# An mLSTM cell followed by a gated MLP on one core: a reordered head, shorter denominators, and seven products for eight in the last chunk

## The chip, the core and the metric

The kernel runs on one core of one Trainium2 chip. The metric is the device time of one execution in microseconds (us); lower is better. Each time below is one of three runs of the kernel before, or belongs to the one execution that the profiler recorded.

The engines are named as in the profile: PE is TensorE (matrix products; PEld its weight loads), DVE is VectorE, ACT is ScalarE, POOL is GpSimd, SP is SyncE, which here does nothing but issue DMA transfers. "Lnnn" is a line of the kernel before, unless a line of the new kernel is meant, which is then said.

## The reference

```python
# q, k, v, o_gate: (4, 8, 768, 40); i_gate, f_gate: (4, 8, 768)
for t in range(S):
    m_new = np.maximum(f_gate[:, :, t] + m, i_gate[:, :, t])
    f_stab = np.exp(f_gate[:, :, t] + m - m_new)
    i_stab = np.exp(i_gate[:, :, t] - m_new)
    m = m_new
    C = f_stab[..., None, None] * C + i_stab[..., None, None] * np.einsum('bhd,bhe->bhde', vt, kt)
    n = f_stab[..., None] * n + i_stab[..., None] * kt
    h_tilde = np.einsum('bhde,bhe->bhd', C, qt)
    denom = np.maximum(np.abs(np.einsum('bhd,bhd->bh', n, qt)[..., None]), 1.0)
    y[:, :, t] = sigmoid(o_gate[:, :, t]) * h_tilde / denom
x = y.transpose(0, 2, 1, 3).reshape(3072, 320)
h = x @ w_in                 # w_in: (320, 2048)
out = (h * np.cos(h)) @ w_out  # w_out: (2048, 320)
```

The two weight matrices arrive as float64 and are made float32 in the kernel from their bits.

## The kernel before

**Cells and chunks.** The 768 steps are cut into 6 chunks of 128 (`c` = 0 to 5), and a chunk into 4 cells, one for each batch entry `b`; cell `n` is chunk `n // 4`, batch `n % 4`, with its 8 heads. A cell turns the recurrence into matrix work: `scores` (L492, keys times queries), `weigh` (L498, times the decays `E`), `values` (L518 to L527, times the values, plus the state carried over times the scaled queries `qG`), `denominators` and `divide` (the normalisation and the output gate), and `seam` and `state`, which bring the state to the next chunk. The four cells of a chunk give `xT[c]` (320 features in 128 + 128 rows, and the remaining 64 twice in `xL[c]`) for the 512 columns of the chunk.

**The MLP.** `Up(c, f2)` makes 256 of the 2048 hidden features for the 512 columns, in two PSUM banks (`pup`, one for `e` = 0, one for `e` = 1): four products over the two 128-row parts (L667, each two instructions) and two over the last 64 rows (L661). Then ACT makes `near` (L675, to integer), DVE `rest` (L678), ACT the sine (L683), DVE `gate` (L687). The banks come free with the last read of `gate`. `down` (L699, chunk 0) or a scheme of 7 products for 8 (L848, chunks 1 to 5, with sums of halves made by DVE and POOL in `sums`, L736 to L744) multiplies the gates by `w_out`.

**The order of the work** is written out by hand: every engine runs its instructions in the order in which the Python text records them. `first_cells` does cells 0 to 3 while data still arrive; `first_period` does cell 4 beside `Up(0, 0)` and `Up(0, 1)`; then `both_parts(c, b)` does the cell `(c + 1) * 4 + b` beside the two slots `f2 = 2b` and `2b + 1` of chunk `c`. A slot is: `Up`, `near`, `rest`, (half a cell), sine and `gate`, and a run of down products. Chunk 5 has no cell beside it.

**Weights.** `w_in` comes in four blocks of 512 features (two slots each), a block in three pieces: `weights_in(f)` issues 4 + 4 transfers of 128 KB (L141) for two 128-row pieces and 4 of 64 KB (L179) for the last rows. `w_out` comes in eight pieces of 640 KB (L185), one for each slot. A piece is made float32 by ACT (`take_apart`, L153 and L155), DVE (`bound`, L159 and L160; then L166) and POOL (`put_together`, L167). `bound` is a clamp and a pair of shifts, both `tensor_scalar` in place. Pieces wait in three (`w_out`) or four (`w_in`) staging buffers called `bits`; a transfer into a buffer waits until POOL has read the piece before it.

**DMA.** SP issues nearly all transfers, one after the other; an instruction there that waits holds all later transfers. Transfers are counted on eight semaphores in turn, so that a transfer also waits for the one eight before it (some of these belong to `seam_out`'s `xL` transfers, which ACT issues, L626). For a cell SP brings `E` (512 KB, broadcast, L369), and for two cells at once the raw queries and keys (L341), `G` (the decays of the state, L358), and keys and values in rows (L346). `load_o` brings the output gates of a chunk (8 transfers of 80 KB, L311), which `sigmoid` (L320, L322) turns; `low_dimensions` (L455, ACT) moves 8 of 40 dimensions of raw queries and keys before DVE can turn them in blocks (`turn_blocks`, L465).

**Normalisation of a turned cell.** `turn_gate` (L470) turns the output gates on DVE; `denominators` (L541, L542) takes max(|d|, 1) over 128 x 128; `divide` multiplies values by gates (L548), takes 128 x 128 reciprocals (L549), spreads two rows over three tiles by three shuffles (L552) and multiplies (L556).

**The gates' tables.** `gates_turn` turns the gate factors of chunks 1 to 5 on PE (L275) after cell 3's values and adds one product (L276); `gates_keep` copies both to SBUF. `clear_low` (L448) sets two raw tiles to zero by POOL in `first_period`. `warm(k)` runs k products (L920) whose results nobody reads.

Of the kernel before, what the change touches and what calls it, by code (L numbers as in the profile page):

```python
# [29 lines left out]
def kernel(  # L30
# [20 lines left out]
    nc = tc.nc  # L51
# [68 lines left out]


# [35 lines left out]
    def bound(dst):  # L157
        t = dst.bitcast(I32)
        nc.vector.tensor_scalar(out=dst, in0=dst, scalar1=LEAST, scalar2=GREATEST, op0=OP.max, op1=OP.min)  # L159
        nc.vector.tensor_scalar(out=t, in0=t, scalar1=5, scalar2=2, op0=OP.logical_shift_left,  # L160
                                op1=OP.logical_shift_right)
# [96 lines left out]
    def gates_exp():  # L258
        for e in (eG, eW):
            nc.scalar.activation(out=e, in_=e, func=AF.Exp)  # L260
        dst = G_d.rearrange("(c j q) s -> j q c s", c=R, j=2)
        for j in range(2):
            nc.gpsimd.dma_start(out=dst[j], in_=eG[j:BH:2])
# [6 lines left out]
    def gates_turn():  # L270
        pg = ps_o.tile([128, R, 2, BH], FP, name="pg", tag="o")
        pd = ps_o.tile([128, R - 1, BH], FP, name="pd", tag="o")
        for c in range(R):
            for j, src in enumerate((a1, eW)):
                nc.tensor.transpose(pg[:, c, j], src[:, c], ident[0:BH, 0:BH])  # L275
        nc.tensor.matmul(pd.rearrange("p c b -> p (c b)"), one.to_broadcast([BH, 128]), dd.rearrange("r c b -> r (c b)"),  # L276
                         start=True, stop=True)
        return pg, pd

    def gates_keep(pg, pd):  # L280
        nc.scalar.copy(out=tab[:, 1:NC, 0:2], in_=pg)
        nc.scalar.copy(out=tab[:, 1:R, 3], in_=pd)
# [163 lines left out]
    def clear_low():  # L446
        for w in "qk":
            nc.gpsimd.memset(raws[w][1], 0.0)  # L448
# [17 lines left out]

    def turn_gate(n):
        c, b = divmod(n, B)
        oTs[n] = p1.tile([128, 3, C], FP, name="oT", tag="oT")
        nc.vector.transpose(out=oTs[n].rearrange("q g (t k) -> q g k t", t=32), in_=sig[c][:, b].rearrange("q (g k) i -> q g k i", g=3))  # L470
# [67 lines left out]
    def denominators(n):  # L538
        vt = heads_of[n]
        dn = dns[n] = p2.tile([128, C], FP, name="dt", tag="dt")  # L540
        nc.vector.tensor_scalar(out=dn, in0=vt[:, 2], scalar1=-TWO_PI, scalar2=TWO_PI, op0=OP.mult, op1=OP.max)  # L541
        nc.vector.scalar_tensor_tensor(out=dn, in0=vt[:, 2], scalar=TWO_PI, in1=dn, op0=OP.mult, op1=OP.max)  # L542

    def divide(n):
        c, b = divmod(n, B)
        vt, dn = heads_of[n], dns[n]
        yt = vt if n == B else p1.tile([128, 3, C], FP, name="yt", tag="yt")
        nc.vector.tensor_tensor(out=yt, in0=vt, in1=oTs[n], op=OP.mult)  # L548
        nc.vector.reciprocal(out=dn, in_=dn)  # L549
        db = p1.tile([128, 3, C], FP, name="db", tag="db")  # L550
        for i, mask in enumerate(([FROM0] * 32, [FROM1] * 32, [FROM0] * 16 + [FROM1] * 16)):
            nc.vector.stream_shuffle(out=db[:, i], in_=dn, mask=mask)  # L552
        if b == 0:
            new_x(c)

        nc.vector.tensor_tensor(out=xT[c][:, NK * b:NK * b + NK + 1], in0=yt, in1=db, op=OP.mult)  # L556
        ys[n] = xT[c][:, NK * b + NK]
# [91 lines left out]
    class Up:  # L649
# [35 lines left out]
        def gate(self, e):  # L685
            g = gp.tile([128, B * C], FP, name="g", tag="g")
            nc.vector.scalar_tensor_tensor(out=g, in0=self.pu[e], scalar=TWO_PI, in1=self.n[e].bitcast(FP),  # L687
                                           op0=OP.mult, op1=OP.mult)
            gs[self.c, 2 * self.f2 + e] = g
# [155 lines left out]
    def run(made, n):  # L845
        for _ in range(n):
            a, lhs, rhs, start, stop = next(made)
            nc.tensor.matmul(a, lhs, rhs, start=start, stop=stop)  # L848
# [39 lines left out]

    def down_slot(c, f2):

        if c == 0:
            if f2 > 0:
                down(0, f2 - 1)
            return
        if f2 == 0:
            if c == 1:
                down(0, LAST)
            else:
                run(made_of[c - 1], 12)
            return  # L900
        if f2 == 1 and c > 1:
            run(late_products(c - 1), NF)
            combine_late(c - 1)
            return
        if c not in made_of:
            made_of[c] = all_products(c) if c < NC - 1 else last_products()
        each = 14 if c == NC - 1 else 12
        quota = [0] * 8
        for m in range(2, 8):
            quota[m] = each * 7 * (m - 1) // 6 - each * 7 * (m - 2) // 6  # L910
        if c == NC - 1:
            quota = [0, 0, 14, 14, 14, 14, 14, 21]
        run(made_of[c], each if c == 1 else quota[f2])
# [8 lines left out]
    def first_cells():  # L922
        nc.vector.memset(nil, 0.0)
        gates_in()
        nc.scalar.copy(out=ident_b, in_=ident)
        load(0, "qk")
# [27 lines left out]
        pieces.extend(weights_in(0))  # L954
# [16 lines left out]
        values(0)  # L971
        normalize(0)
        scores(1)
        gates_exp()
        turn(2)
        turn_out(2, False)
        warm(2)
        seam(0)
        weigh(1)
        seam_out(0)  # L980
        state(0)
        load_two(B, "qk")
# [5 lines left out]
        load_M(B)  # L988
        outs.append((0, weights_out(0)))
# [24 lines left out]
        pg = gates_turn()  # L1014
        warm(2)
        more = weights_in(1)
        pieces.append(next(more))
        load_G(B)
        load_two(B, "Kv")
# [6 lines left out]
        bound(pieces[0][0])  # L1026
        put_together(*pieces.pop(0))
        gates_keep(*pg)
        pieces.extend(more)
        load_M(B + 1)  # L1030
# [3 lines left out]
        load_E(B + 2)  # L1034
        low_dimensions(B)
# [5 lines left out]
        odd_values(B)  # L1041
# [17 lines left out]
    def first_period():  # L1059
# [16 lines left out]
        for some in pieces:  # L1076
            take_apart(*some)
        out_of_psum(n)
        bound(piece[0])
        put_together(*piece)  # L1080
        load_out(p)
        up = Up(0, 1)
        for dst, bits in pieces:
            bound(dst)
            put_together(dst, bits)
        pieces.clear()
        for e in range(2):
            up.near(e)
# [12 lines left out]
        clear_low()  # L1101
# [3 lines left out]
        load_out(p)  # L1105
# [3 lines left out]
        turn_gate(n)  # L1109
# [3 lines left out]
        pieces.extend(weights_in(2))  # L1113
        load_two(n + 2)
        load_E(n + 3)
# [6 lines left out]
    def both_parts(c, b):  # L1122
# [3 lines left out]
        for i in range(2):  # L1126
            f2 = 2 * b + i
            up = Up(c, f2)
# [9 lines left out]
            if i == 0:  # L1138
# [14 lines left out]
                if c == 0:  # L1153
                    made = [pieces.pop(0) for _ in range(min(1, len(pieces)))]
                    p, piece = outs.pop(0)
                    made.append(piece)
                    for dst, bits in made:
                        take_apart(dst, bits)
                    for dst, bits in made:
                        bound(dst)  # L1160
                    for dst, bits in made:
                        put_together(dst, bits)
                    load_out(p)
# [27 lines left out]
            if cell and i == 0:  # L1191
                turn_gate(n)
                values(n)
                seam(n)
                normalize_turned(n)
                fade(n)
# [14 lines left out]
            if i == 1:  # L1211
# [14 lines left out]
                if (c, f2) == (0, LAST):  # L1226
                    weight_sums(0)

# [39 lines left out]
```

## Time and profile before

| what | value |
|---|---|
| three runs | 531.06, 528.66, 533.04 us; median 531.06 us |
| the profiled execution | 532.28 us, of which the span of its instructions is 530.5 us |
| mean granted clock of PE in it | 0.987 |
| busy: PE, DVE, ACT, POOL | 512.6, 426.3, 285.5, 227.9 us |
| DMA | 57.81 MB, mean 109 GB/s over the span |
| PE work that nothing interrupts | from about 91 us to about 526 us |

The first 91 us are the head, in which the data of eight cells and most of the weights arrive. A row of a timeline has start, duration, engine, line, operation, `out<-in`, shape and count, and in brackets how long the engine had been idle and what ended that. SPq and ACTq rows are transfers being issued, their duration includes any waiting inside the issue. In a table of windows each engine's busy time is followed by its number of instructions; then come the granted clock of PE (1.00 is full), the busy share of the DMA engines and GB/s.

### The profile page before, as it was taken

The numbers are of one execution on the slowest core, as the hardware profiler recorded it, in microseconds if no ns is written. First come the engines' busy times: TensorE is split into PE (matmuls) and PEld (weight loads), VectorE is DVE, ScalarE is ACT, GpSimd is POOL, SyncE is SP. The second block draws the span as 40 slices with busy tenths as digits, with TensorE's granted clock in tenths as the row PEclk, the third lists the DMA queues.
The fourth block names the chain that finished last, engine by engine and source line by source line (L and its number), as shares of the span: only waits on it lengthen the run. The fifth ranks groups of instructions, "written<-read, shape, count | busy, mean of one in ns | idle before, by whom it ended". The sixth has DMA issues, their size and how long they took to land.

```text
span 530.5 us, 10499 instructions
## 1 busy us (share of the span) xinstructions
PE 512.6 (97%) x3844; PEld 348.6 (66%) x3844; DVE 426.3 (80%) x908; ACT 285.5 (54%) x546; POOL 227.9 (43%) x369
## 2 busy tenths in 40 slices
PE   7997987999999999999999999999999999999997
PEld 4874554556657666677677667667667667575666
DVE  5888989997879888898878898878898878664645
ACT  2888668757656537745537736526826522222230
POOL 7544545653785663533532632632421421221211
PEclk9988997999999999999999999999999999999999
DMA  9999879878939259149159239159210000010001
GB/s 138 215 223 186 215 214 233 176 145 231 179 122 184 59 119 176 42 107 182 45 116 159 51 92 177 38 127 171 46 65 7 2 5 6 5 47 1 0 1 49
DMA packets 99939, 57.81 MB, mean 109 GB/s; under 512 B 62304, under 2 KB 92608, under 8 KB 99888
## 3 DMA queue, kind: packets, MB, share of 16 engines
q1 hardware_dynamic: 96352, 55.48, 49.4%
q10 hardware_dynamic: 3392, 1.49, 1.4%
q8 instruction: 30, 0.49, 0.4%
q14 instruction: 21, 0.17, 0.1%
q0 software_dynamic: 144, 0.18, 0.1%
HBM read 51.71 MB, written 4.11 MB: 105 GB/s over the span
## 4 chain that ended last, share of the span: by engine, by line
PE 79%; DVE 8%; DMA 5%; POOL 2%; ACT 2%; SPq 1%; issue 1%; DVEq 0%; POOLq 0%; ACTq 0%
PE pup L667 27%; PE acc L848 24%; PE pup L661 8%; PE po L699 4%; PE late L848 3%; PE ps L492 3%; PE vt L527 2%; PE vt L518 2%; DMA bits<-in_moe_w_out_dram 2%; DMA G<-G_d 2%; PE pu L619 1%; PE ph L508 1%; DMA bits<-in_moe_w_in_dram 1%; PE pw L920 1%; DVE g L687 1%
## 5 line engine op out<-in xcount | busy, mean ns | idle before, releaser
L667 PE MATMUL pup<-xT,w_in_sb 128*128 128x512 f32 x384 | 175.4, 600 | 0.2
L675 ACT ACTIVATE n<-pup 128x512 int32<-128x512 f32 x96 | 53.7, 594 | 184.8 <-PE pup L661 132.7
L667 PEld LDWEIGHTS pup<-xT,w_in_sb 128*128 128x128 f32 x384 | 70.2, 191 | 85.6 <-issue 83.4
L678 DVE SCALAR_TENSOR_TENSOR n<-pup,n 128x512 f32<-128x512 f32 x96 | 62.9, 687 | 67.6 <-ACT n L675 66.4
L741 POOL TENSOR_TENSOR D<-g 128x128 f32<-128x128 f32 x40 | 19.8, 495 | 214.2 <-DVE g L687 214.2
L683 ACT ACTIVATE n<-n 128x512 f32<-128x512 f32 x96 | 57.9, 628 | 24.1 <-DVE n L678 17.1
L687 DVE SCALAR_TENSOR_TENSOR g<-pup,n 128x512 f32<-128x512 f32 x96 | 61.7, 684 | 3.9 <-ACT n L683 3.3
L848 PE MATMUL acc<-w_out_sb,g 128*128 128x160 f32 x320 | 59.0, 306 | 0.0
L848 PE MATMUL acc<-T,g 128*128 128x160 f32 x304 | 55.0, 301 | 0.0
L661 PE MATMUL pup<-xL,w_in_l 64*128 64x512 f32 x192 | 54.2, 642 | 0.0
L848 PEld LDWEIGHTS acc<-w_out_sb,g 128*128 128x128 f32 x320 | 47.7, 190 | 8.7 <-issue 7.2
L413 ACT ACTIVATE E<-E,tab 128x128 f32<-128x128 f32 x160 | 49.0, 388 | 0.3
L848 PEld LDWEIGHTS acc<-T,g 128*128 128x128 f32 x304 | 45.8, 190 | 1.8 <-issue 1.4
L699 PE MATMUL po<-w_out_sb,g 128*128 128x320 f32 x128 | 39.3, 464 | 4.4 <-POOL w_out_sb L167 4.4
L699 PEld LDWEIGHTS po<-w_out_sb,g 128*128 128x128 f32 x128 | 25.7, 204 | 17.3 <-POOL w_out_sb L167 5.4
L848 PE MATMUL acc<-T,S 128*128 128x160 f32 x160 | 34.8, 300 | 0.0
L492 PEld LDWEIGHTS ps<-t,t 40*128 40x128 f32 (+1 forms) x384 | 24.6, 188 | 12.0 <-DVE t L465 6.5
L498 DVE TENSOR_TENSOR E<-ps,E 128x512 f32<-128x512 f32 x48 | 30.7, 680 | 0.0
L661 PEld LDWEIGHTS pup<-xL,w_in_l 64*128 64x128 f32 x192 | 14.5, 185 | 22.9 <-issue 21.2
L474 POOL TENSOR_TENSOR qG<-t,G 128x512 f32<-128x512 f32 x20 | 25.7, 1283 | 8.8 <-DVE E L498 4.3
L848 PE MATMUL acc<-w_out_sb,S 128*128 128x160 f32 x160 | 28.8, 299 | 0.0
L848 PEld LDWEIGHTS acc<-T,S 128*128 128x128 f32 x160 | 26.3, 191 | 1.4 <-issue 1.4
(194 smaller groups left out, 887.4 us busy)
## 6 DMA issues: line engine op xcount, KB each, us to landing
E<-M_d SPq DMA_DIRECT2D x22, 512.0 KB
qr<-in_q_dram SPq DMA_DIRECT2D x36, 160.0 KB
kr<-in_k_dram SPq DMA_DIRECT2D x36, 160.0 KB
bits<-in_moe_w_out_dram SPq DMA_DIRECT2D x8, 640.0 KB
G<-G_d SPq DMA_DIRECT2D x20, 256.0 KB
bits<-in_moe_w_in_dram SPq DMA_DIRECT2D x32, 128.0 KB
out_dram<-o_sb SPq DMA_DIRECT2D x23, 160.0 KB
ks<-in_k_dram SPq DMA_DIRECT2D x10, 320.0 KB
```

The costliest lines, as they stand in the source:

```text
L413: nc.scalar.activation(out=Es[n][:, h], in_=Es[n][:, h], func=AF.Exp, scale=-1.0, bias=tab[:, c, 0, g:g + 1])
L474: nc.gpsimd.tensor_tensor(out=qG, in0=qkT[n][0], in1=Gs[n], op=OP.mult)
L492: nc.tensor.matmul(ps[j][:, p], kT[r, p], qT[r, p], start=True, stop=True)
L498: nc.vector.tensor_tensor(out=w, in0=pss[n][j], in1=w, op=OP.mult)
L661: nc.tensor.matmul(pu, w_in_l[r, f2], xL[c][r].rearrange("p b t -> p (b t)"), start=ahead, stop=not ahead)
L667: nc.tensor.matmul(pu.rearrange("p (b t) -> p b t", b=B), w_in_sb[:, i, ts(2 * f2 + e, 128)], xT[c][:, i:NK * B:NK], start=(i == 0 and not ...
L675: nc.scalar.activation(out=self.n[e], in_=self.pu[e], func=AF.Copy, bias=0.25)
L678: nc.vector.scalar_tensor_tensor(out=self.n[e].bitcast(FP), in0=self.pu[e], scalar=0.25, in1=self.n[e], op0=OP.add, op1=OP.subtract)
L683: nc.scalar.activation(out=r, in_=r, func=AF.Sin, scale=TWO_PI_DOWN)
L687: nc.vector.scalar_tensor_tensor(out=g, in0=self.pu[e], scalar=TWO_PI, in1=self.n[e].bitcast(FP), op0=OP.mult, op1=OP.mult)
L699: nc.tensor.matmul(po[c][b], gs[c, f][:, ts(b, C)], w_out_sb[:, f], start=(f == 0), stop=(f == NF - 1))
L848: nc.tensor.matmul(a, lhs, rhs, start=start, stop=stop)
```

## The change

1. **First cells.** `clear_low` moves to ACT, right behind the copy of `ident_b`: four copies of an already cleared tile (partitions 32 to 63 and 64 to 127 of both raw tiles, 1312 elements each). `gates_turn` moves from behind cell 3's values to cell 2, where `warm(2)` was; its second half stays behind cell 3 as `gates_spread`, followed by `warm(6)` in place of `warm(2)`.
2. **Transfers of the head.** Raw queries and keys, `G`, keys and values are loaded for cell 4 alone and, later, for cell 5 alone (twice as many transfers of half the size), and stand ahead of `w_out`'s first piece. `E` of cell 4 goes in between block 0's pieces. Block 1's first two pieces come at once, before `E` of cell 5. Block 2 of `w_in`, `E` of cell 6 and raw queries and keys of cells 6 and 7 are issued in the middle of `first_period`, ahead of `w_out`'s pieces 3 and 4; before, they stood behind them at its end.
3. **Clamps.** For the last piece of block 0 and the three of block 1 `bound` uses `scalar_tensor_tensor` with a broadcast one-column tile as second input.
4. **ACT's order.** `low_dimensions_of(n + 1)` for cell 5 stands before the copy `out_of_psum(n)` in `first_period`. In chunk 0's slots the piece of `w_out` is taken before that of `w_in`.
5. **Denominators.** A 128 x 128 block transpose, then max and reciprocal over 128 x 8; the reciprocals are multiplied into the output gates in place, which are then turned, and one product with the values ends it.
6. **Last chunk.** `UpFast` takes 7 products of half the columns for the 8 that four full products amount to, with sums of weights (POOL, during chunk 4) and of inputs (POOL, once), two ACT copies out of PSUM between the products, and five additions for each slot on POOL and DVE. `fill_in` runs two down products between the first four and the last three of the seven (not in the first two slots); the slot's own run of down products is two shorter.

```diff
+    def clear_low():
+        for w in "qk":
+            for r in (slice(32, 64), slice(64, 128)):
+                nc.scalar.copy(out=raws[w][1][r], in_=raws[w][0][r])
...
+    def bound(dst, beside=False):
...
+        if beside:
+            nc.vector.scalar_tensor_tensor(out=dst, in0=dst, scalar=LEAST, in1=greatest.to_broadcast(list(dst.shape)), op0=OP.max, op1=OP.min)
+            nc.vector.scalar_tensor_tensor(out=t, in0=t, scalar=5, in1=two.to_broadcast(list(dst.shape)), op0=OP.logical_shift_left,
+                                           op1=OP.logical_shift_right)
+            return
...
     def denominators(n):
-        nc.vector.tensor_scalar(out=dn, in0=vt[:, 2], scalar1=-TWO_PI, scalar2=TWO_PI, op0=OP.mult, op1=OP.max)
-        nc.vector.scalar_tensor_tensor(out=dn, in0=vt[:, 2], scalar=TWO_PI, in1=dn, op0=OP.mult, op1=OP.max)
+        nc.vector.transpose(out=d, in_=heads_of[n][:, 2].rearrange("q (t k) -> q k t", t=32))
+        nc.vector.scalar_tensor_tensor(out=dn, in0=both, scalar=-TWO_PI, in1=least.rearrange("q (k g) -> q k g", g=2), op0=OP.mult, op1=OP.max)
+        nc.vector.scalar_tensor_tensor(out=dn, in0=both, scalar=TWO_PI, in1=dn, op0=OP.mult, op1=OP.max)
+        nc.vector.reciprocal(out=dn, in_=dn)
     def divide(n):
-        nc.vector.tensor_tensor(out=yt, in0=vt, in1=oTs[n], op=OP.mult)
-        nc.vector.reciprocal(out=dn, in_=dn)
-            nc.vector.stream_shuffle(out=db[:, i], in_=dn, mask=mask)
+        nc.vector.tensor_tensor(out=o[:, 0:2], in0=o[:, 0:2], in1=..., op=OP.mult)
+        nc.vector.tensor_tensor(out=last, in0=last, in1=..., op=OP.mult)
+        nc.vector.transpose(out=oT.rearrange("q g (t k) -> q g k t", t=32), in_=o)
-        nc.vector.tensor_tensor(out=xT[c][:, NK * b:NK * b + NK + 1], in0=yt, in1=db, op=OP.mult)
+        nc.vector.tensor_tensor(out=xT[c][:, NK * b:NK * b + NK + 1], in0=vt, in1=oT, op=OP.mult)
...
+    class UpFast(Up):
+            product(b1, second, S2, T2, True, True)
+            product(b1, first, S3, X[0][1], stop=True)
+            product(b0, first, A11, X[0][0], True, True)
+            product(b0, second, S1, T1, stop=True)
+            nc.scalar.copy(out=s[:, 2:4], in_=b1.rearrange("p (k n) -> p k n", k=2))
+            nc.scalar.copy(out=s[:, 0:2], in_=b0.rearrange("p (k n) -> p k n", k=2))
+            fill()
+            product(b1, first, A22, T4)
+            product(b0, first, A12, X[1][0])
+            product(b0, second, S4, X[1][1])
...
+            nc.gpsimd.tensor_tensor(out=s[:, 1], in0=s[:, 1], in1=s[:, 0], op=OP.add)
+            nc.vector.tensor_tensor(out=s[:, 0], in0=s[:, 0], in1=s[:, 3], op=OP.add)
+            nc.gpsimd.tensor_tensor(out=s[:, 3], in0=s[:, 1], in1=s[:, 2], op=OP.add)
+            nc.vector.tensor_tensor(out=b0[:, second], in0=b0[:, second], in1=s[:, 0], op=OP.add)
+            nc.vector.tensor_tensor(out=h, in0=b1.rearrange("p (k n) -> p k n", k=2), in1=h, op=OP.add)
...
     (first_cells, cell 1)
+        load_M(B)
+        pieces.extend(first)
+        load_blocks(B)
     (cell 2)
         gates_exp()
+        load_G_of(B)
         turn(2)
         turn_out(2, False)
-        warm(2)
+        gates_turn()
         seam(0)
+        load(B, "kv")
+        outs.append((0, weights_out(0)))
     (behind cell 3's values)
-        pg = gates_turn()
-        warm(2)
+        pd = gates_spread()
+        warm(6)
         more = weights_in(1)
-        pieces.append(next(more))
-        load_G(B)
-        load_two(B, "Kv")
+        pieces.extend(next(more) for _ in range(NK))
+        load_M(B + 1)
...
     (first_period)
         for some in pieces:
             take_apart(*some)
+        low_dimensions_of(n + 1)
         out_of_psum(n)
...
         for dst, bits in pieces:
-            bound(dst)
+            bound(dst, True)
             put_together(dst, bits)
         pieces.clear()
+        more = weights_in(2)
+        pieces.append(next(more))
+        load_M(n + 2)
+        pieces.extend(more)
+        load_two(n + 2, "qk")
+        load_out(p)
...
     (both_parts, chunk 0)
-                    made = [pieces.pop(0) for _ in range(min(1, len(pieces)))]
                     p, piece = outs.pop(0)
-                    made.append(piece)
+                    made = [piece, *(pieces.pop(0) for _ in range(min(1, len(pieces))))]
```

## The prediction

> **What bounds the kernel now.** I read the busy times, then a table of windows, then the timelines of PE and of whatever PE waits for.
>
> ```profile
> PE 512.6 (97%) x3844; PEld 348.6 (66%) x3844; DVE 426.3 (80%) x908; ACT 285.5 (54%) x546; POOL 227.9 (43%) x369
> 45.40:52.20 6.80, 3.17 (x58) 2.77 (x56) 6.66 (x10) 5.04 (x9) 4.88 (x4) 0.75 0.81 179
> 66.00:79.50 13.50, 11.65 (x116) 7.23 (x113) 10.96 (x23) 8.81 (x18) 5.47 (x4) 1.00 0.80 214
> 79.50:91.00 11.50, 8.55 (x20) 5.09 (x19) 10.46 (x27) 10.72 (x24) 6.41 (x7) 0.70 1.10 216
> 112.00:450.00 338.00, 337.09 (x2723) 231.37 (x2722) 284.82 (x630) 183.90 (x350) 149.58 (x250) 1.00 0.50 103
> 450.00:521.00 71.00, 71.00 (x345) 47.43 (x344) 42.69 (x80) 18.98 (x34) 16.43 (x36) 1.00 0.03 10
> ```
>
> PE is the bound from 91 us on: 337.09 of 338 us, then 71 of 71. There only less PE work saves time. PE stands still or runs at half clock only in the head, in two places:
>
> ```profile
> 49.25 0.66 PE L518 MATMUL vt<-E,vs 128*32 128x128 f32 x8 [3.62 <-ACT bits L155]
> 76.90 3.70 PE L667 MATMUL pup<-xT,w_in_sb 128*128 128x512 f32 x8
> 83.55 7.58 PE L699 MATMUL po<-w_out_sb,g 128*128 128x320 f32 x16 [2.94 <-POOL w_out_sb L167]
> 90.97 3.60 PE L667 MATMUL pup<-xT,w_in_sb 128*128 128x512 f32 x8
> ...
> 49.17 0.86 POOL L424 COPY vr<-vs 128x128 f32<-128x128 f32 x1 [1.04 <-DMA vs<-in_v_dram]
> ...
> 76.50 0.66 ACT L153 ACTIVATE w_in_sb<-bits 128x512 f32<-128x512 f32 x1 [2.95 <-DMA bits<-in_moe_w_in_dram]
> 61.83 1.28 ACT L320 ACT_TABLE_LOAD   x1 [0.44 <-DMA o<-in_o_gate_dram]
> ...
> 62.53 6.48 SPq L185 DMA_DIRECT2D bits<-in_moe_w_out_dram  x2
> 69.07 8.35 SPq L141 DMA_DIRECT2D bits<-in_moe_w_in_dram  x8
> ```
>
> First place: cell 4's values wait until 49.25; the row names ACT, but POOL's row shows the true releaser, the transfer of `vs`, landed at 49.1. Second: `down(0, 2)` waits 2.94 us for `w_out`'s piece 2 and then takes 7.58 us for what takes 4.58 elsewhere (68.67), at granted clock 0.50 after the gap. Piece 2 was late because ACT took block 2 of `w_in` first and that landed at 76.4; it was late because SP stood 6.48 us before `w_out`'s piece 4, whose buffer piece 1 still held.
>
> **The change, part by part**, against the profiled execution (532.28 us, span 530.5); it lies 1.2 us above the median of 531.06, so I subtract 1.2 at the end.
>
> *Cells 0 to 3.* Four copies on ACT: 1024 elements take 1.06 us (L320), 128 take 0.39 (L413), so 1312 some 1.3 each, 5.2 in all, in ACT's idle time from 2.8 us on. Behind them waits e0's exponential (5.12), now at about 8.0 and done at 8.4; PE turns it at 8.93 behind `warm`. Two tiny memsets put 0.1 before the first scan. `gates_turn` (ten rows, 0.65) now waits for the exponential that ends at 21.07, so `seam(0)` goes from 21.59 to about 21.8; its copy (0.43) fits ACT's idle 0.43 there. Behind cell 3 four more `warm` (0.21 to 0.41 each) replace those rows, ahead of a `seam` that waits for DVE until 36.0. Together 0 to +1; I take 0, since what follows waits for transfers, not PE.
>
> *Cell 4's transfers.* Through `vs` the queue has carried 6.5 MB instead of 8.5. At the 174 to 225 GB/s of the rows around, 2 MB are 9 to 11 us, so they land before 40. Next late is `weigh(4)` (DVE, done at 46.3). Values start 2.9 us earlier, and their block costs 1.7 as at 73.64 instead of 3.04 at half clock: `Up(0, 1)` 4.2 us earlier. Little of it passes on: DVE stands next with `w_out` piece 0 and the three clamped pieces, and `Up(0, 2)` needs the banks that `gate(0, 1)` frees behind them.
>
> *Clamps.* These rows decide:
>
> ```profile
> 50.35 1.68 DVE L160 TENSOR_SCALAR w_in_sb<-w_in_sb 128x512 int32<-128x512 int32 x1
> 85.31 0.43 DVE L160 TENSOR_SCALAR w_in_sb<-w_in_sb 128x512 int32<-128x512 int32 x1
> 67.73 1.29 DVE L548 TENSOR_TENSOR vt_s<-vt_s,oT 128x384 f32<-128x384 f32 x1
> 84.17 0.56 DVE L556 TENSOR_TENSOR xT<-yt,db 128x384 f32<-128x384 f32 x1
> ```
>
> The old form takes 0.43 alone and 1.68 beside POOL's L167 (50.02 to 51.75). The new form has no row; L166, also with two inputs, takes 0.69 for 512 and 0.42 for 256. Four instructions of each size cost 4 x 0.26 + 4 x 0.13 = +1.6 us; if they wait for POOL no more, the waits of 37.95 to 56.8 (0.76 + 0.77 + 1.25 + 0.97 + 1.04) go, 4.8, and the balance is -3.2. A two-input instruction with both inputs in SBUF does wait in this trace: L548 took 1.29 beside L167 (67.05 to 68.61), the like-sized L556 0.56 alone. So I take +1.6, which eats DVE's earlier start (ACT takes the first piece at about 47 instead of 48): `gate(0, 1)` ends about where it did, `Up(0, 2)` starts 0.5 us earlier. The Trainium skill ("SBUF — State Buffer", section "SBUF: two separate sides") speaks against the new form too: a VectorE instruction with two SBUF inputs takes the pair of ports it shares with GpSimd as well, and the later one waits out the other. The trace agrees, with 1.29 beside 0.56; were it not so here, DVE would be 4.8 us ahead of this sum at that point.
>
> *ACT's order.* Ahead of cell 4's copy (53.35) ACT now moves cell 5's low dimensions (four copies, at most 1.66 as at 38.24 to 39.9), for which cell 5's keys must have landed. From 34.25 on SP issues 2.1 MB up to them, with some 1 MB in flight: at 174 to 225 GB/s they land at 48 to 52. ACT gets there at about 50.5, so it waits 0 to 2; I take 0. `Up(0, 1)` ends near 52.2, so `near` is not held.
>
> *The output gates.* The transfers ahead of them are the same set in another order, 11.1 MB. Only idle time of the queue can move their landing from 61.8. Eight more issues at 0.5 (L341) are 4 us of SP's time, mostly while it would wait. I take -1.3 (bounds -3 and +2). `sigmoid`, the table loads and `decay(5)` follow on ACT (6.5 us as now), then `near(0, 2)`: 67.0 instead of 68.26.
>
> *Denominators.* DVE's rows from 66.83 to 71.57 (4.7 us) become two products, a turn of 0.87 and a product of 0.56 to 0.90; beside POOL, whose L167 and L474 hold them up, about 4. `rest(0, 2)` starts at 69.9 instead of 71.6; `Up(0, 3)` at 74.7 instead of 75.84: -1.1 (bounds +1 and -4). In chunks 1 to 4 the saving of about 1 us a cell lies beside a saturated PE: 0.
>
> *Block 2 first.* Its issue no longer stands behind piece 4; behind the output gates, 2.5 MB at 214 GB/s (the row 66.00:79.50) land by 72, the first piece by 67. ACT takes `w_out` piece 2 at 72, DVE and POOL (0.97, 0.86, 0.82, 1.57) finish it at 77.7; `Up(0, 3)` ends at 79.3, so `down(0, 2)` does not wait and runs at full clock: 83.8. Next late is ACT: `decay(6)`, a piece and a table put `near(0, 3)` at 81.3, `gate` ends at 85.2. `Up(0, 4)` starts at 85.3 instead of 90.97: **-5.7** for the whole head (bounds -3, if PE's new gap of 1.5 us costs the clock again, and -7.5, if the gates land 3 us sooner). SP now stands behind `xL` of cell 4 before cell 6's raw data; the last block of `w_in`, needed by ACT at 92.5 (98.2 now), should land near 90.
>
> *Chunk 4.* POOL makes the weight sums: four instructions of 1024 elements, twice the 1.27 of L474, 10 us on an engine at 43%. The `S` sums on DVE may wait 2.5 at a time, with a slot in hand: 0 (bounds 0, +1.5). PE's 0.9 us of idle bounds a gain.
>
> *Last chunk.*
>
> ```profile
> 501.81 3.60 PE L667 MATMUL pup<-xT,w_in_sb 128*128 128x512 f32 x8
> 505.33 1.13 PE L661 MATMUL pup<-xL,w_in_l 64*128 64x512 f32 x4
> 506.39 0.81 PE L848 MATMUL acc<-w_out_sb,g 128*128 128x160 f32 x4
> ```
>
> L667 x8 takes 3.52 us from start to start, 0.44 for 512 columns; L848 takes 0.14 for 160 (28 in 3.91); so 256 cost about 0.2215. 14 x 0.2215 = 3.10 saves 0.42 a slot, 3.35 in eight. Between the products stand two ACT copies (0.58 each, L479). The second ends 2.5 us after the slot's start; with the fill of 0.57 PE gets there at 2.8, without it (two slots) it waits 0.5: +1.0. Afterwards DVE adds 0.4 and 0.69 before `near`, so `gate` for `e` = 0 ends 8.0 us after the slot's start and is needed 0.9 after the next one, at 8.9: a slack of 0.8. **-2.35** (bounds 0, -3.35).
>
> Sum: -5.7 - 2.35 = -8.05, so 524.2 for the profiled execution, **523.0** for the median.
>
> **Rivals.**
> 1. *The head is bound by the gates' landing anyway.* If they land 2 us later, or DVE's two-input work waits longer for POOL, `Up(0, 4)` gains about 1 us: 531.06 - 1 - 2.35 = 527.7. For it: the same bytes, and DMA's share 0.81 to 1.10. Against it: the second gap came from SP's wait of 6.48, which goes.
> 2. *The last chunk doesn't pay.* Copies and additions take the 0.8 of slack and the slot stays 8.49 us: 531.06 - 5.7 = 525.4. For it: five more steps in the loop. Against: ACT is busy 19 of 71 us there.
> 3. *Slower: ACT stands before cell 5's keys.* `near(0, 1)` comes 1.8 us after their landing; now it is at 56.7. Each us of landing beyond 55 costs a us, and the gains of 8 are used up at 63; at 69 the time is 537. For it: ACT runs in order and all of chunk 0 follows. Against: 3.1 MB in the 29 us to 63 are 108 GB/s, half of what the rows show.
>
> **Numbers.** Forecast 0.56, first rival 0.23, second 0.14, third 0.07. A measurement of this kernel can tell about 1% from no change, 5.3 us. The forecast ends below 525.7 in 0.5 of its 0.56, the first rival in 0.03, the second in 0.08: faster 0.61. Slower by over 1% is most of the third rival, 0.05; the rest is 0.34. The range, 518.0 to 529.5, runs from the bounds -7.5 and -3.35, with 2 us for the spread of runs, to the first rival with the same 2.
>
> **What would show it.** Right: no wait for `vs` near 49, `down(0, 2)` at about 4.5 us without a wait for POOL, `Up(0, 4)` near 85, and slots of 8.1 us in the last chunk. Wrong: ACT idle before the low dimensions; new clamps under 0.8 us beside POOL's L167; the sigmoid still at 62 or later; PE waiting for Sx copies.

## The result and the profile after

| | median | range | runs | ratio to before, 95% interval |
|---|---|---|---|---|
| before | 531.41 us | 528.66 to 533.26 | 20 | |
| after | 533.80 us | 532.07 to 539.39 | 20 | 1.0052 [1.0032, 1.0072] |

The changed kernel is 0.5% slower, 2.4 us by the medians; 523.0 was forecast. The profiled execution of after took 534.89 us (span 533.1); that of before 532.28 (span 530.5). The lines below are of after, and its line numbers are those of the new file: L714 and L708 are `Up` (L667 and L661 before), L833 `down`, L550 the product of values in cells 0 to 3, L418 the decay mask, L428 its exponential, L540 `weigh`, L461 `turn`, L184 `put_together`, L734 `gate`, L780 the products of `UpFast`, L789 its second copy out of PSUM, L1065 `warm`. The nine fastest of the twenty runs of after, 532.07 to 533.43 us, have a mean granted clock of PE of 0.987 and the other eleven, the profiled one among them, 0.978 to 0.984, so that its profile shows more half clock than those nine had.

First the busy times and a table of windows of after (columns as before: PE, PEld, DVE, ACT, POOL, granted clock, DMA share, GB/s).

```profile
PE 514.8 (97%) x3894; PEld 358.9 (67%) x3894; DVE 426.4 (80%) x854; ACT 301.1 (56%) x570; POOL 250.5 (47%) x393
```

```profile
24.00:28.00 4.00, 4.00 (x56) 3.66 (x56) 1.45 (x6) 0.14 (x2) 1.09 (x2) 1.00 1.01 234
28.00:30.00 2.00, 0.21 (x10) 0.08 (x4) 0.51 (x1) 1.58 (x2) 1.38 (x2) 1.00 0.73 246
30.00:34.00 4.00, 3.32 (x28) 3.23 (x30) 3.90 (x9) 3.94 (x7) 2.01 (x2) 0.78 0.57 120
34.00:45.40 11.40, 11.40 (x66) 8.01 (x65) 6.15 (x16) 5.95 (x17) 2.47 (x3) 0.50 0.71 182
```

From 24 to 28 us ACT does 0.14 us of work; from 28 to 30 PE does 0.21; and from 34 to 45.4 PE is listed as busy throughout, but at half clock. None of the three is in the profile of before: there PE is busy in every stretch from 22 to 45 us, and at half clock from 35.1 to 38.5 only. What started the first two is in POOL's timeline of after:

```profile
21.20 1.10 POOL L280 DMA_DIRECT2D G_d<-kr  x2
26.91 0.42 POOL L313 MEMSET qs<- 128x384 f32 x1 [4.61 <-PE pt L461]
27.28 1.09 POOL L418 TENSOR_SCALAR_AFFINE_SELECT E<-E 128x1024 f32<-128x1024 f32 x1
28.34 1.04 POOL L437 TENSOR_TENSOR kw<-ks,tab 128x512 f32<-128x512 f32 x1
```

then in those of ACT and DVE:

```profile
28.41 1.06 ACT L428 ACTIVATE E<-E 128x1024 f32<-128x1024 f32 x1 [4.26 <-POOL E L418]
29.49 1.29 DVE L540 TENSOR_TENSOR E<-ps,E 128x512 f32<-128x512 f32 x2 [2.73 <-ACT E L428]
```

and in that of PE:

```profile
27.70 0.51 PE L666 MATMUL pu<-vs,kw 128*40 128x48 f32 x16
30.24 1.98 PE L550 MATMUL ph<-vs,E 128*128 128x41 f32 x16 [2.03 <-DVE E L540]
32.66 2.17 PE L534 MATMUL ps<-t,t 64*128 64x128 f32 x16 [0.44 <-DVE dn L615]
...
37.42 3.64 PE L550 MATMUL ph<-vs,E 128*128 128x41 f32 x16
40.99 0.79 PE L296 MATMUL pd<-dd,one 32*128 32x128 f32 x2
41.72 2.74 PE L1065 MATMUL pw<-nil 128*128 128x512 bf16 x6
```

The MEMSET is an instruction that the prediction does not have. `load(B, "kv")` is meant to load only keys and values, but `load` evaluates `qs(n)` for its table of three before it looks at `which`, and `qs` takes a query tile for cells 4 and 5 and has POOL zero 384 columns of it. The tile comes from the same pool of two buffers as `G`. `load_G_of(B)`, recorded earlier, has already taken the buffer that cells 0 and 1 gave back, so the tile gets the one that still holds the queries of cells 2 and 3, and POOL waits until PE has turned them (`turn(3)`, L461). Nobody reads the tile. Behind it on POOL stands the decay mask of cell 2: it starts at 27.28, in before at 23.41, +3.9. ACT's exponentials, DVE's weighing and PE's L550 follow. PE then waits 2.03 and 0.44 us, and works at half clock from 32.3 to 45.9, where the second L550 takes 3.64 us for 1.98. The first `Up` starts at 46.07 instead of 37.87. That the wait brings on the half clock is not shown: e1 below has a spell of half clock from 23.9 to 30.8 without a wait of PE longer than 0.26 us in the 9 us ahead of it, and e12 has none in this stretch.

The starts of some `Up` in us (`Up(c, f2)`; 133.5 is the beginning of chunk 1):

| profile of | Up(0,0) | Up(0,2) | Up(0,4) | Up(0,6) | Up(1,0) | span |
|---|---|---|---|---|---|---|
| before | 37.9 | 61.7 | 91.0 | 112.1 | 133.5 | 530.5 |
| after | 46.1 | 68.4 | 93.4 | 117.0 | 138.9 | 533.1 |

The 8.2 us of delay shrink to 2.5 at `Up(0,4)`, so a gain is there too; they are 5.4 at chunk 1, 4.4 at chunk 5, and 2.6 at the end, by the last chunk.

### The profile page after: what moved, and what is told of

Same layout as the page of the kernel before. It is cut to its first block, busy times and chain, and to the rows that moved or that the text cites. A ratio compares the mean times of both kernels' runs of the same rounds, so it can differ in the third digit from the quotient of the medians.

```text
span 533.1 us, 10600 instructions
## 1 busy us (share of the span) xinstructions
PE 514.8 (97%) x3894; PEld 358.9 (67%) x3894; DVE 426.4 (80%) x854; ACT 301.1 (56%) x570; POOL 250.5 (47%) x393
## 4 chain that ended last, share of the span: by engine, by line
PE 72%; DVE 4%; issue 1%; DMA 1%; POOL 1%; SPq 1%; ACT 1%; DVEq 0%; POOLq 0%; ACTq 0%
PE acc L982 24%; PE pup L714 21%; PE pup L708 6%; PE pup L780 4%; PE late L982 3%; PE ps L534 3%; PE po L833 2%; PE vt L569 2%; PE vt L560 2%; PE pup L796 2%; PE pu L666 1%; DVE t L512 1%; PE vt L563 1%; PE vt L566 1%; DMA qr<-in_q_dram 1%
## 5 line engine op out<-in xcount | busy, mean ns | idle before, releaser
L714 PE MATMUL pup<-xT,w_in_sb 128*128 128x512 f32 x320 | 149.9, 612 | 6.3 <-DVE g L734 6.3
L722 ACT ACTIVATE n<-pup 128x512 int32<-128x512 f32 x88 | 49.8, 593 | 155.7 <-PE pup L708 86.6
L714 PEld LDWEIGHTS pup<-xT,w_in_sb 128*128 128x128 f32 x320 | 59.0, 193 | 82.9 <-issue 78.1
L725 DVE SCALAR_TENSOR_TENSOR n<-pup,n 128x512 f32<-128x512 f32 x88 | 58.1, 686 | 50.0 <-ACT n L722 48.5
L734 DVE SCALAR_TENSOR_TENSOR g<-pup,n 128x512 f32<-128x512 f32 x88 | 56.7, 682 | 2.5 <-ACT n L730 1.9
L708 PE MATMUL pup<-xL,w_in_l 64*128 64x512 f32 x160 | 45.2, 641 | 0.0
L833 PE MATMUL po<-w_out_sb,g 128*128 128x320 f32 x128 | 36.2, 436 | 0.0
L540 DVE TENSOR_TENSOR E<-ps,E 128x512 f32<-128x512 f32 x48 | 30.6, 679 | 3.4 <-ACT E L428 3.4
L833 PEld LDWEIGHTS po<-w_out_sb,g 128*128 128x128 f32 x128 | 24.0, 190 | 11.3 <-issue 1.7
L184 POOL TENSOR_TENSOR w_out_sb<-w_out_sb,bits 128x640 int32<-128x640 int32 x8 | 13.6, 1696 | 33.0 <-issue 13.2
L534 PE MATMUL ps<-t,t 40*128 40x128 f32 (+1 forms) x384 | 27.3, 282 | 1.1 <-DVE t L512 0.5
```

Of the source, the lines that this page charges most:

```text
L534: nc.tensor.matmul(ps[j][:, p], kT[r, p], qT[r, p], start=True, stop=True)
L540: nc.vector.tensor_tensor(out=w, in0=pss[n][j], in1=w, op=OP.mult)
L708: nc.tensor.matmul(pu, w_in_l[r, f2], xL[c][r].rearrange("p b t -> p (b t)"), start=ahead, stop=not ahead)
L714: nc.tensor.matmul(pu.rearrange("p (b t) -> p b t", b=B), w_in_sb[:, i, ts(2 * f2 + e, 128)], xT[c][:, i:NK * B:NK], start=(i == 0 and not ...
L722: nc.scalar.activation(out=self.n[e], in_=self.pu[e], func=AF.Copy, bias=0.25)
L725: nc.vector.scalar_tensor_tensor(out=self.n[e].bitcast(FP), in0=self.pu[e], scalar=0.25, in1=self.n[e], op0=OP.add, op1=OP.subtract)
```

## The experiments

All times are medians, with the range, beside runs of the kernel before on the same chip (531.74, 531.29 and 531.63 us in the three groups: e1 to e4, e5 to e8, e9 to e12). The groups ran on three chips, so runs of different groups are compared by their ratios too. No run is numbered e10.

| run | us | range | runs | ratio to before, 95% interval |
|---|---|---|---|---|
| e1: after, no zeroing | 528.32 | 527.24 to 531.72 | 9 | 0.9954 [0.9934, 0.9974] |
| e4: e1 with one-input clamps | 526.74 | 526.23 to 530.78 | 12 | 0.9932 [0.9911, 0.9952] |
| e8: after, one-input clamps, zeroing kept | 533.77 | 531.03 to 534.72 | 12 | 1.0036 [1.0017, 1.0056] |
| e12: after, zeroing behind cell 2 | 528.68 | 527.08 to 531.78 | 12 | 0.9947 [0.9927, 0.9968] |
| e2: before plus zeroing | 531.52 | 530.61 to 532.24 | 12 | 0.9998 [0.9986, 1.0009] |
| e5: the same, `G` taken first | 530.95 | 530.00 to 533.39 | 12 | 0.9994 [0.9979, 1.0009] |
| e9: the same, zeroing that waits | 535.54 | 534.31 to 537.68 | 6 | 1.0074 [1.0048, 1.0100] |
| e3: before plus the last chunk's change | 529.72 | 528.17 to 532.67 | 12 | 0.9966 [0.9948, 0.9984] |
| e7: e4 with the old last chunk | 528.37 | 527.68 to 531.28 | 8 | 0.9941 [0.9921, 0.9960] |
| e6: e4 with the old denominators | 530.06 | 527.56 to 531.25 | 10 | 0.9965 [0.9945, 0.9985] |
| e11: e4 with the old order of blocks | 529.39 | 528.09 to 531.58 | 12 | 0.9961 [0.9943, 0.9980] |

**Theory**: POOL's wait for `turn(3)` in front of the unused tile's zeroing, and what is queued behind it, costs some 5 us. **Rivals**: the two-input clamps, the last chunk or the reordered head cost them.

### e1: the tile is taken only when it is loaded

```diff
-        for name, dst, src in (("q", qs(n), q), ("k", ks(n), k), ("v", vs(n), v)):
+        for name, tile_of, src in (("q", qs, q), ("k", ks, k), ("v", vs, v)):
             if name in which:
-                nc.sync.dma_start(out=dst[:, :, 0:D], ...)
+                nc.sync.dma_start(out=tile_of(n)[:, :, 0:D], ...)
```

> The changed kernel, but the row loads of cells 4 and 5 (keys and values) no longer allocate and zero a tile for queries that is never used. Theory A (that zeroing on POOL, which waits 4.6 us for PE's turning of cell 3's queries, holds back cell 2's decay mask, and so PE, which then falls to half clock until Up(0, 0)): Up(0, 0) starts near 38 instead of 46.1, no half clock from 34 to 45, and the time is 5 to 8 us below the changed kernel's 533.8: 526 to 529. Rival B (the half clock comes from the gates' turning and the warm products that were moved, the zeroing only adds its own wait): at most 2 us better, 532 or more, half clock still there. Rival C (the head is bound by the transfers and the clamped pieces anyway): Up(0, 0) near 38, but Up(0, 2) still at 66 or later, and 531 to 533.

528.32 us: 5.5 below after (5.2 by the ratios), 3.4 below before. The profiled execution took 531.10 us, 2.8 above its median; in it `Up(0,0)` starts at 40.2, and there is no half clock from 34 to 45. POOL's mask of cell 2 in e1, with nothing ahead of it:

```profile
23.09 1.09 POOL L418 TENSOR_SCALAR_AFFINE_SELECT E<-E 128x1024 f32<-128x1024 f32 x1 [1.44 <-DVE E L417]
```

One evaluated name turned the change's gain into a loss.

### e2, e5, e9: the zeroing put into the kernel before

The same instruction in before, in three ways: as it is (e2); with `G`'s tile taken first, but not written (e5); with one column of it written, so that it holds its buffer (e9). In e5 and e9 `load_G` of cell 4, not shown, fills this early tile instead of taking one.

```diff
         gates_exp()
+        early_G.append(p2.tile([128, 2 * HP, C], FP, name="G", tag="G"))     # e5, e9
+        nc.vector.memset(early_G[0][:, 0, 0:1], 0.0)                          # e9
         turn(2)
         ...
         seam(0)
+        qs(B)                                                                 # e2, e5, e9
```

> The kernel before with only that one tile allocated and zeroed on POOL, behind cell 0's seam. Theory A: cell 2's mask comes some 4 us later there too, Up(0, 0) at 44 to 46 instead of 37.9, and the time 3 to 8 us above before: 534 to 539. Rival B: under 2 us, since the gates and the warm products stand where they stood. Rival C: Up(0, 0) late, but most of it is taken up before Up(0, 4), under 2 us.

> The kernel before, with the query tile of cell 4 allocated and zeroed behind seam(0), and the buffer of cell 4's gates taken ahead of it, so that the zeroing gets the buffer that holds the queries of cells 2 and 3 and has to wait for TensorE's turn(3), as in the changed kernel. The tile is not used. Theory A (the wait of POOL, not the zeroing, costs the time): the decay mask of cell 2 starts 3 to 4 us later than 23.4, TensorE stands about 2 us before cell 2's scores are weighed and falls to half clock, the first Up starts 4 to 8 us later than 37.9, and the time is 2 to 6 us above the kernel before (533.5 to 537.5). Theory B (the late start of the first Up has another cause in the changed kernel): within 1 us of the kernel before.

> The run with the waiting zeroing in the kernel before once more, since the zeroing got the free buffer there and didn't wait: now VectorE writes one column of the gates' tile behind the gates' exponents, so that this tile really holds the free buffer and the zeroing gets the buffer of cells 2 and 3. The tile is not used otherwise. Theory A (the wait of POOL costs the time by itself): the zeroing runs at 26 to 27, the decay mask of cell 2 starts at 26.5 to 27.5 instead of 23.4, the first Up starts 3 to 8 us later than 37.9, and the time is 2 to 6 us above the kernel before (533.5 to 537.5). Theory B (it costs only together with the other changes): within 1 us of the kernel before, though the mask starts late.

In e2 and e5 the zeroing got the free buffer and did not wait, and nothing changed; so neither answers the question of the wait, but both price the instruction itself at nothing. POOL's rows in e5:

```profile
21.68 0.44 POOL L294 MEMSET qs<- 128x384 f32 x1
23.13 1.09 POOL L405 TENSOR_SCALAR_AFFINE_SELECT E<-E 128x1024 f32<-128x1024 f32 x1 [1.01 <-DVE E L404]
```

and in e9:

```profile
27.41 0.42 POOL L294 MEMSET qs<- 128x384 f32 x1 [4.40 <-PE pt L448]
27.78 1.09 POOL L405 TENSOR_SCALAR_AFFINE_SELECT E<-E 128x1024 f32<-128x1024 f32 x1
```

and PE in e9:

```profile
30.74 1.98 PE L514 MATMUL ph<-vs,E 128*128 128x41 f32 x16 [2.03 <-DVE E L504]
33.16 1.76 PE L498 MATMUL ps<-t,t 64*128 64x128 f32 x16 [0.44 <-DVE dn L574]
...
42.80 4.26 PE L673 MATMUL pup<-xT,w_in_sb 128*128 128x512 f32 x8
```

With the wait, e9 has after's pattern, to the 2.03 and 0.44 us, and takes 535.54 us: 3.9 more than before. Its mask starts 4.4 us later than in before and its first `Up` 4.9, with two spells of half clock (33.7 to 37.1 and 40.5 to 43.9). The wait alone is enough for most of the loss, without the other changes.

### e12: the zeroing kept, but nothing urgent behind it

```diff
         seam(0)
-        load(B, "kv")
...
         weigh_k(2)
+        load(B, "kv")
```

> The changed kernel with the loads of cell 4's keys and values, and so the zeroing, moved behind the weighing of cell 2's keys; the zeroing stays, it takes the same buffer, and the two-input clamps stay. Theory A (what costs is the decay mask of cell 2, queued on POOL behind the zeroing that waits): like the changed kernel without the zeroing, 527.5 to 529, with the first Up at 38 to 40.5. Theory B (the zeroing or the unused tile costs by itself): 532 or more.

528.68 us, as e1. The first `Up` starts at 37.2 and `Up(0,4)` at 85.5. The zeroing waits 1.07 us for the same transposes, and costs nothing, as cell 2's mask has gone ahead; POOL in e12:

```profile
23.20 1.09 POOL L418 TENSOR_SCALAR_AFFINE_SELECT E<-E 128x1024 f32<-128x1024 f32 x1 [1.44 <-DVE E L417]
24.26 1.04 POOL L437 TENSOR_TENSOR kw<-ks,tab 128x512 f32<-128x512 f32 x1
26.38 0.42 POOL L313 MEMSET qs<- 128x384 f32 x1 [1.07 <-PE pt L461]
```

So it is neither the instruction nor the buffer, but the mask behind it in POOL's queue.

### e4 and e8: the clamps

```diff
-            bound(dst, True)
+            bound(dst)
...
-        bound(pieces[0][0], True)
+        bound(pieces[0][0])
```

> The first of these, with the clamps of the last piece of block 0 and of block 1 as tensor_scalar again. If a two-input clamp waits for POOL as the one-input form does (L173 of the changed kernel: 1.95, 1.67, 1.39), the two-input form costs about 0.26 for 512 and 0.13 for 256, 1.6 in eight instructions, and this kernel is 0 to 1.6 us faster than the first. If the two-input form helps, it is 1 to 3 us slower.

> The changed kernel with one-input clamps and nothing else changed: the zeroing and its wait stay. Theory A (the zeroing costs about 5, the two-input clamps 1.6, and they add): 531.5 to 532.5. Theory B (the two share one slack: once the first Up is late, the landing of the gates and clamps don't matter): 533 to 534, no better than the changed kernel.

Without the zeroing one-input clamps gain 1.6 us of the median (526.74, the fastest kernel of all: 5.0 below before, 7.1 below after), 1.2 by the ratios, whose intervals overlap. With it e8's median, 533.77, is after's, so by medians theory B of e8 holds; by the ratios it is 0.8 faster, which the intervals do not separate. The lowest runs say otherwise: 532.07 and 531.03 with the zeroing, 527.24 and 526.23 without, so 4.8 for the zeroing in both pairs and 1.0 for the clamps in both. So the two-input clamps cost 1.0 to 1.6 without the zeroing, a size that is not settled; whether the zeroing hides it is open. DVE's rows of three clamped pieces, here in after:

```profile
56.92 0.68 DVE L172 SCALAR_TENSOR_TENSOR w_in_sb<-w_in_sb,greatest 128x512 f32<-128x512 f32 x1
57.64 1.95 DVE L173 SCALAR_TENSOR_TENSOR w_in_sb<-w_in_sb,two 128x512 int32<-128x512 int32 x1
...
60.95 1.67 DVE L173 SCALAR_TENSOR_TENSOR w_in_sb<-w_in_sb,two 128x512 int32<-128x512 int32 x1
...
63.71 1.39 DVE L173 SCALAR_TENSOR_TENSOR w_in_l<-w_in_l,two 128x256 int32<-128x256 int32 x1
```

and the same three pieces on DVE in e4:

```profile
49.62 0.42 DVE L176 TENSOR_SCALAR w_in_sb<-w_in_sb 128x512 f32<-128x512 f32 x1
50.08 1.68 DVE L177 TENSOR_SCALAR w_in_sb<-w_in_sb 128x512 int32<-128x512 int32 x1
...
52.86 1.39 DVE L177 TENSOR_SCALAR w_in_sb<-w_in_sb 128x512 int32<-128x512 int32 x1
...
55.22 1.33 DVE L177 TENSOR_SCALAR w_in_l<-w_in_l 128x256 int32<-128x256 int32 x1
```

The long row of either form stands beside POOL's `put_together` (57.14 to 59.03 in after, 49.84 to 51.48 in e4) and ends shortly behind it, 0.56 and 0.28 us; the first 512-column piece costs 2.63 us in the new form, 2.10 in the old. The one-input form is held up beside POOL too (1.68 us, where the row at 85.31 in before has 0.43 for the same).

### e3 and e7: the last chunk alone, and the rest alone

e3 puts `UpFast`, its sums and its fill into before; e7 takes them out of e4:

```diff
-            up = Up(c, f2)
+            up = UpFast(c, f2, lambda: fill_in(c, f2)) if c >= fast else Up(c, f2)
```

> The kernel before with the last chunk's seven products for eight alone. By the forecast's step (0.42 us a slot, less what two slots without a fill wait) 2.35 us less than before: 529.0; by the changed kernel's trace (chunk 5 starts 4.4 us later and ends 2.6 later) 1.8 less: 529.6. Rival: the weight sums on POOL during chunk 4 cost as much as it saves, 531 or more.

> The fastest kernel so far (526.74) with the last chunk's Up as before, eight blocks for eight: what is left is the head's change with one-input clamps. Theory A (gains of head and tail add up: the last chunk alone was worth 2.0 in the kernel before): 528.7, that is 2.7 below the kernel before, and the tail begins as early as in the fastest kernel. Theory B (the head's lead is eaten on the way, and the 5.0 us come from the tail in good part): 530.5 or more.

e3: -2.0 us (interval of the ratio: -0.8 to -2.8). e7: -2.9 against before where e4 has -5.0, which leaves 2.1 to the last chunk. So about -2 come from the tail and -2.9 (interval -2.1 to -4.2) from all the rest, with one-input clamps, and the two add up.

### e6: lean denominators undone

`denominators`, `divide` and `turn_gate` are those of before; the two calls come back:

```diff
         decay(n + 1)
+        turn_gate(n)
         divide(n)
...
             if cell and i == 0:
+                turn_gate(n)
                 values(n)
```

> The fastest kernel so far (the changed kernel without the zeroing and with one-input clamps, 526.74) with the denominators, their spreading and the division as before the change. Theory A (lean denominators save little, since their small two-input instructions stand beside POOL's work at 1.2 us): within 0.8 us of it, 526 to 527.5. Theory B (the prediction: 1.1 us in front of Up(0,3) and again in each later group): 1 to 3 us slower, 527.7 to 529.7.

530.06 us, 3.3 above e4 by the medians and 1.8 by the ratios, whose intervals overlap; the lowest runs differ by 1.3, the two profiled spans by 0.7. It is slower, but the size is not settled. The place is not the prediction's: with the old form `Up(0,3)` starts at 73.6 (e4 73.8), `Up(1,0)` at 129.8 (e4 130.7), and then e6 loses 0.2 to 0.6 in every chunk and is 0.7 behind at chunk 5 (447.7 and 447.0). All profiles agree on this: from the start of chunk 1 to that of chunk 5 the six with the old form (before, e2, e3, e5, e6, e9) take 317.36 to 317.89 us, the seven with the lean form 316.33 to 316.54. In front of `Up(0,3)` the lean form does save DVE's time: from the first row of `denominators` to `rest(0,2)` e4 takes 8.10 us and e6 8.90. But PE does not wait for it there: between the starts of `Up(0,2)` and `Up(0,4)` its only wait, in e4 and in e6, is the one right in front of `Up(0,4)`. And where the smallest instructions of the lean form stand beside POOL they are no longer small. DVE in after, a group of them alone and a group beside POOL's L184 (83.40 to 85.29 and 85.25 to 86.54):

```profile
69.24 0.17 DVE L587 SCALAR_TENSOR_TENSOR d<-dt,least 128x8 f32<-128x8 f32 x1
69.44 0.17 DVE L588 SCALAR_TENSOR_TENSOR d<-dt,d 128x8 f32<-128x8 f32 x1
...
84.12 1.19 DVE L587 SCALAR_TENSOR_TENSOR d<-dt,least 128x8 f32<-128x8 f32 x1
85.35 1.22 DVE L588 SCALAR_TENSOR_TENSOR d<-dt,d 128x8 f32<-128x8 f32 x1
```

### e11: the old order of the two blocks in chunk 0

```diff
-                    p, piece = outs.pop(0)
-                    made = [piece, *(pieces.pop(0) for _ in range(min(1, len(pieces))))]
+                    made = [pieces.pop(0) for _ in range(min(1, len(pieces)))]
+                    p, piece = outs.pop(0)
+                    made.append(piece)
```

> The fastest kernel so far (526.74, lowest run 526.23) with the order of the two blocks of output and input weights in chunk 0 as before: the block of w_in first, the block of w_out behind it. Theory A (the prediction: the wait of down(0,2) for its block comes back, about 2 us, and the head loses 3 us or more): 529 to 530, down(0,2) with a wait of 1.5 us or more for POOL. Theory B (VectorE's chain bounds the head there, and gives back what down(0,2) gains): within 1 us of 526.7.

529.39 us, 2.65 above e4 (1.5 by the ratios, whose intervals overlap, 1.9 by the lowest runs): the time of theory A, but not its place. PE in e11:

```profile
78.67 4.47 PE L833 MATMUL po<-w_out_sb,g 128*128 128x320 f32 x16
85.25 3.67 PE L714 MATMUL pup<-xT,w_in_sb 128*128 128x512 f32 x8 [2.11 <-DVE g L734]
...
104.39 4.58 PE L833 MATMUL po<-w_out_sb,g 128*128 128x320 f32 x16 [0.55 <-POOL w_out_sb L184]
111.23 5.37 PE L714 MATMUL pup<-xT,w_in_sb 128*128 128x512 f32 x8 [2.26 <-DVE g L734]
```

`down(0,2)` (78.67) does not wait, and `Up(0,4)` is at 85.25, 0.4 behind e4. The loss comes one group later: `w_out` is late there, `gate` too, and `Up(0,6)` runs at half clock, 2.4 us behind e4. So the order of the two blocks is not what frees `down(0,2)`; the earlier transfers and the rest of the head are left, which no run takes apart.

## Why the prediction was wrong, step by step

**Cells 0 to 3: "together 0 to +1; I take 0."** This is the step that failed. It costed what the diff adds, but not what a called function does: loading "kv" for cell 4 also takes and zeroes a query tile on POOL. POOL was not in the step at all. Its rule, "what follows waits for transfers, not PE", was wrong as well: a delay of 3.9 us of a mask became 8.2 us at `Up(0,0)`. A part of this is half clock. With a mask 4.4 us late e9 has its `Up(0,0)` 4.9 us late, and 5.7 us of half clock ahead of it; after has 13.7. As an estimate, each us at 0.50 costs half a us, so the 8 us more cost after some 4 us, of which 3.3 are seen (8.2 less 4.9). Price of the step: 5.5 us by medians, 5.2 by ratios, 4.8 by lowest runs (e1), 3.9 in before (e9).

**Block 2 first: "Up(0, 4) starts at 85.3 instead of 90.97: -5.7 for the whole head."** Without the zeroing's wait the time is right: 84.83 in e4 and 85.5 in e12 (88.6 in e1's profile), and `down(0, 2)` does not wait, in after either (86.93, 4.47 us). In after itself `Up(0, 4)` is at 93.4. "For the whole head" is wrong. PE in e4 from there on:

```profile
78.37 4.47 PE L833 MATMUL po<-w_out_sb,g 128*128 128x320 f32 x16
84.83 3.67 PE L714 MATMUL pup<-xT,w_in_sb 128*128 128x512 f32 x8 [1.99 <-DVE g L734]
...
90.96 1.16 PE L534 MATMUL ps<-t,t 40*128 40x128 f32 x16 [1.39 <-DVE t L512]
...
108.80 3.67 PE L714 MATMUL pup<-xT,w_in_sb 128*128 128x512 f32 x8 [1.05 <-DVE g L734]
...
114.05 1.16 PE L534 MATMUL ps<-t,t 40*128 40x128 f32 x16 [0.52 <-DVE t L512]
```

From `Up(0,4)` to `Up(0,6)` e4 takes 24.0 us and before 21.1. From `Up(0,4)` to chunk 1 PE now waits for DVE three times, 2.96 us in all, where in before it does not wait, and 6.1 us of lead are 2.8 at chunk 1; in e12 5.5 become 1.6. The prediction named ACT as next late at `Up(0,4)` and looked no further; in e4 it was DVE all four times. Besides, the profiled execution of before was late at that place: with the same code there, e3 has `Up(0,4)` at 88.8 and e5 at 87.8. What is left of the change without the last chunk is -2.9 with one-input clamps (e7), and -1.4 with the two-input ones (e1's -3.4 less e3's -2.0). About 1.0 of either is won in chunks 1 to 4 (e6), so the head itself is worth some -1.9 and -0.4, for -5.7.

**Clamps: "+1.6".** Right in kind and nearly in size. The new form waits for POOL (1.95, 1.67, 1.39), three pieces cost DVE 6.80 us for 5.52, +1.3, and the kernel perhaps 1.0 to 1.6. This is what the section "SBUF: two separate sides" of the Trainium skill's page "SBUF — State Buffer" would have it do.

**Denominators: `Up(0, 3)` -1.1, and "in chunks 1 to 4 ... 0".** Both places are wrong. DVE gains 0.8 us in front of `Up(0,3)`, near the 0.7 of the sum, but PE does not wait for DVE there; and in each of the chunks 1 to 4, where nothing was taken, the gain is 0.2 to 0.6 us, 0.8 to 1.6 in all (e6 and the other profiles). How it reaches PE there is open.

**Cell 4's transfers.** Right that the wait for `vs` goes; little passed on, as said. **ACT's order.** Right, 0: the copies for cell 5 had no wait, at 58.75 in after and at 50.72 in e12. **Output gates**: in after ACT comes to the sigmoid 7 us later than before, when the gates have landed; in e4 and e12 it comes at 60.25 and 60.81 and does not wait, so that they had landed by then, as forecast (60.5). **Chunk 4**: right; it takes 79.16 us in e3 with the weight sums and 79.15 in before.

**Last chunk: -2.35.** Nearly right: -2.0 alone (e3), and from the start of chunk 5 to the end every profile with `UpFast` takes 77.8 to 77.9 us, every other one 79.6 to 79.7, so -1.8. A slot with a fill takes 8.08 us for 8.49; PE in after at the start of three slots, with the waiting product of the first slot above them:

```profile
457.80 0.70 PE L780 MATMUL pup<-xT,w_in_sb 128*128 128x256 f32 x2 [0.16 <-ACT Sx L789]
...
496.67 0.59 PE L780 MATMUL pup<-Tx,kr 128*128 128x256 f32 x2
...
504.75 0.59 PE L780 MATMUL pup<-Tx,kr 128*128 128x256 f32 x2
...
512.83 0.59 PE L780 MATMUL pup<-Tx,kr 128*128 128x256 f32 x2
```

The first two slots, without a fill, take 8.05 and 9.13 us for 7.95 and 9.03: they lose their 0.42 and 0.10 more, 1.0 in all, as taken, though only 0.16 each is listed as a wait. What was overlooked is the last slot: from its start to the end after takes 20.3 us and before 20.2, so its 0.42 does not show.

The sum: by e1 the forecast's own terms come to -3.4 for -8.05, mostly because the head's lead is lost again behind `Up(0,4)`, and the missed step, which is after less e1, adds 5.5. Without the missed step the time would have been within the range, by terms less than half as large as forecast. The first rival (527.7) was nearest to e1's 528.32, and it named DVE's two-input work waiting for POOL; but it has the lead lost ahead of `Up(0,4)`, where the traces have it lost behind. No rival had what happened in after. The range's own terms give 518.2 to 529.7, for 518.0 to 529.5.

## What to carry to other kernels

Cost an edit by the instructions it issues, not by its text: a helper called for part of its work may still take a buffer and clear it, and on a pool of two that means a wait for the last reader of the other buffer, with all that is queued behind it. When a stall is taken away, follow the chain for two or three more uses and add up the other engines' waits, as a lead at one place is not a lead at the end. Take a lead from several executions: one profile of a head with gaps may be 2 to 3 us off at a place.

## What the runs showed of the hardware

Half-clock spells of PE have lengths of one step of 3.4 us and its multiples, in every profile here (up to 140 us): 35.1 to 38.5 in before (3.4), 23.9 to 30.8 in e1 and 34.5 to 41.3 in e5 (6.8), 32.3 to 45.9 in after and 31.7 to 45.4 in e8 (13.6 to 13.7), none before 59 us in e4 and e12. The Trainium skill's page "TensorE: Matmul & The Clock Gate" (section "Part 1: The HAM clock gate (the "warmup" mystery)") has a free-running window of about 3.4 us, so that spells differ from execution to execution; the lengths here agree. What starts and ends a spell is not shown.

PE listed as busy without a break did not bring the clock back at once: from 34 to 45.4 us in after it was busy 11.40 of 11.40 us, with small float32 products and eight `warm` instructions (128x512 bf16), at 0.50.

A DVE instruction of 8 columns with two inputs took 1.19 us beside POOL for 0.17 alone, and ended with POOL's instruction (85.31 and 85.29); one of 512 columns took 1.95 for 0.69. What is added in these rows is about what remained of POOL's instruction (1.17 of 1.89 us and 1.39 of 1.89), not a share of DVE's own length.
